# A fused attention and gated block on one core: w_phi loaded in 200-byte runs and placed by selection products, x tile 0 in halves, and a new order of work

## The chip, the cores and the metric

The kernel runs on one core of one Trainium2 chip. A core has five engines with instruction streams of their own: TensorE (PE, matrix products; its weight loads are shown apart as PEld), VectorE (DVE), ScalarE (ACT), GpSimd (POOL) and SyncE (SP, which here only issues transfers). Sixteen DMA engines move data; transfers are issued from SP's queue or from ScalarE's. The metric is the time of one execution on the device, in microseconds, as the median of several runs.

## The reference

x has 2048 rows of 640 columns; there are 32 heads of 20 columns, and F is 1536. All inputs are bf16.

```python
def A(x, wqkv, w_phi, wo):                # x is the layernorm of A_x
    q, k, v = split(x @ wqkv)             # 32 heads x 20
    pq, pk = q @ w_phi[h], k @ w_phi[h]   # 20 x 20 for each head
    phi_q = concat(softmax(pq), softmax(-pq))
    phi_k = concat(softmax(pk), softmax(-pk))
    kv, z = phi_k.T @ v, sum(phi_k)
    o = (phi_q @ kv) / (phi_q @ z + 1e-6)
    return merge_heads(o) @ wo

def B(x, w_gate, w_up, w_down):           # x is the layernorm of h
    return ((x @ w_gate) * (x @ w_up)) @ w_down

h  = x + A(layernorm(x), ...)
h2 = h + B(layernorm(h), ...)
```

## The kernel before

Rows are cut into 16 tiles t of 128; the 640 columns into five chunks c of 128 (`NC`). `build_graph` makes one `Op` for every piece of work, with its engine, the buffers it reads and writes, and a closure that emits the instructions; `G.op` takes its place from the table `PLAN`: a key that orders it on its engine, the number of the engine among the alternatives (`:1` moves it to the other one, for example a copy from ScalarE to VectorE, or a load from SP's queue to ScalarE's), and its buffer slots. `arrange` sorts each engine's operations by key, `emit` works out which semaphores each must wait for, and `program` emits them. So every queue runs strictly in the order of the table, and an operation that waits holds up all that stands behind it on its engine.

The stages, with the names that the text uses:

- **Loads** (`dma`, `xload`, `wrows`, `wqt`): x0, x1, x3 (one tile each), x4 to x14 (two tiles each), wk0 to wk4 and wv0 to wv4 (row chunks of the K and V parts of wqkv), w5 (w_phi as five chunks of 128 rows of 20 columns, that is 640 runs of 40 bytes), wqt0 to wqt4 (transposing loads of the Q part), wo, wg, wu, wd (the other weights).
- **Warm products** (L367, L372): `warm0` to `warm21` multiply a tile of zeros, eight first and then `NFILL` = 14, spread between the first real products.
- **Folds.** GpSimd multiplies w5 by a mask GL into the three block tensors Phi (`Ph0` to `Ph2`, L380). TensorE transposes the chunks of wk (`WT0` to `WT4`, L392), a copy brings each to SBUF (`WTe`), and the fold `F1_i` (L411) multiplies it with Phi, so that K is projected straight to pk; `Fe1_i` copies the result to `Wp` (L251). `F0_i` does the same for Q from wqt, once all five wqt are there.
- **Layernorm of x**: `L1s`, `L1a` (VectorE statistics), `L1l`, `L1e` (ScalarE), `xn` (L453). Tiles 0 and 1 are transposed by TensorE (`xt0`, `xt1`, L462; copies `xte`), the others by a transposing DMA from SP (`xt`, L471).
- **Projections** (L482): `K`, `V`, `Q` of a tile, ten products of about 320 columns each; for tiles 0 and 1 cut in five pieces of two products (`K0_0` to `K0_4`), by chunk of the weights.
- **Features of K**: two exponentials (`Kx`, L494), sums (`Ks`, L498), logarithm and exponential (`Kr`, `Ke`), the scaling (`Kn`, L518); then `KV` (L526), eleven products of 63 columns, accumulated over the 16 tiles. `KVe` masks the sum into KVm.
- **Q side**: `Qx`, `Qs`, `Qr`, `Qb`, `Qe`, `Qn`, and the transposing DMA `qT` (L575, on SP).
- **Output of attention**: `N` (L588, eleven products), division (`dd`, `rd`, `o`), transposing DMA `oT` (L619, on SP), `O` (L625), then `h`, `hc`, and the transposing DMA `hT` (L653, on SP).
- **Gated block**: row blocks 0 to 4 of 256, 512, 512, 512, 256 rows. `U{block}_{ft}_{0 or 1}` (L668) are the gate and up products, `g` and `u` their evacuation, `D{tile}_0` (L687) the down products, `y` the sum with the residual (L699), `w` the store (L701). The last tile, 15, is cut in three column pieces, `D15_0` (320), `D15_1` (224) and `D15_2` (96).

After the first folds the order on TensorE mixes the stages: K and V run with folds of Q and KV between them, the first N come after KV15, and the first U after O0 and O1.

Of the kernel before, what the change touches and what calls it, by code (L numbers as in the profile page):

```python
# [8 lines left out]
ALU = mybir.AluOpType  # L9
AX = mybir.AxisListType  # L10

P = 128
# [35 lines left out]
NFILL = 14  # L48
# [5 lines left out]
x1:0.78:1 ekz:0.78 x0:0.78 zero:0.91 id0:1.014 warm0:1.127 id1:1.252 x3:1.26:1 wk3:1.26:1 warm1:1.345 va1:1.496 warm2:1.564 w5:1.74:1 warm3:1.782 warm4:2.001  # L54
warm5:2.219 wk0:2.22:1 eps:2.326 gl0:2.357 warm6:2.437 gla:2.518 warm7:2.656 wk4:2.7:1 glb:2.822 warm8:2.874::0 warm9:3.093 wk1:3.18 warm10:3.311 warm11:3.529
wk2:3.66:1 L1s1:3.725 warm12:3.748 warm13:3.966 x4:4.14 warm14:4.185 warm15:4.403 L1s0:4.512 wv1:4.62 warm16:4.621 warm17:4.84 wv0:5.1:1 L1a1:5.299 L1s3:5.408
WT3:5.446::1 L1l1:5.532 wv2:5.58:1 Ph2:5.775 L1e1:5.858 warm18:5.902 warm19:6.011 wv3:6.06 WTe3:6.1:1 warm20:6.12 L1a0:6.195 xn1:6.304::0 Ph1:6.369 x2:6.54
WT0:6.546::2 L1l0:6.685 Ph0:6.761 L1a3:6.834 xt1:6.971::3 wv4:7.02:1 WTe0:7.023:1 L1l3:7.067 L1e0:7.249 WT4:7.25::4 L1e3:7.393 xte1:7.486 xn0:7.487::1 x6:7.5
L1n3:7.673 WT1:7.746::5 phz:7.897 WTe4:8.017:1 warm21:8.025 F1_0:8.134::6 WTe1:8.223:1 xn3:8.425::2 F1_3:8.453::0 WT2:8.772::2 Fe1_0:8.808:1 xt0:9.051::3
xt3:9.063 WTe2:9.249:1 F1_1:9.33::4 Fe1_3:9.392 F1_4:9.649::6 xte0:9.657:1 Fe1_1:9.976 L1s4:10.065 F1_2:10.153::0 x8:10.373 K0_0:10.472::2 Fe1_2:10.67:1  # L60
K0_1:10.743 L1s5:10.852 wqt4:10.853 K1_0:11.014::4 Fe1_4:11.254:1 K1_1:11.285 K1_2:11.556 L1a4:11.639 L1a5:11.762 V1_0:11.827::0 L1l4:11.995 K1_3:12.098
# [12 lines left out]
L1n10:34.156:1 L1a13:34.331 xn11:34.44::3 Kr4:34.517 Ve7:34.663::7 L1a15:34.97 xt11:35.078 L1a12:35.079 K9:35.091::6 Ks7:35.188::2 Ke4:35.247 Kx6_0:35.393::4
Kx6_1:35.977 Kn4:36.316 wd0:36.388 Q0_0:36.447::0 L1l12:36.561 Ks6:36.713::0 Q0_1:36.719 Kx9_0:36.743::1 Q0_2:36.991 Q0_3:37.263 Kr7:37.327 Q0_4:37.535
Ke7:37.618 L1e12:37.764 Q1_0:37.807::2 Kx9_1:37.857 Q1_1:38.079 xn10:38.106::2 Q1_2:38.351 Kr6:38.441 Q1_3:38.623 mk2:38.629 L1n12:38.636:1 Ke6:38.732
Ks9:38.811::3 Q1_4:38.895 L1n15:38.9 Kn6:39.123 KV4:39.167 Qx1_0:39.365::0 K8:39.5::6 Qx1_1:39.975 L1n13:40.204:1 xn13:40.488::0 Qx0_0:40.585::1 KV5:40.856
Qs1:41.018 xt13:41.126 Q5:41.189::2 Qx0_1:41.195 Kn7:41.437 Kx8_0:41.805::2 Kx8_1:42.389 xt10:42.436 xn15:42.453::1 K11:42.556::0 Kr9:42.973 Qx5_0:43.119::2
Ks8:43.125::1 Qr1:43.729::0 xt15:43.746 Ke9:43.875 KV6:43.912 Qx5_1:44.021 Qb1:44.073 Q3:44.245::6 Kn9:44.272 Qs0:44.518 Kx11_0:44.631::3 wu2:45.056
Kx11_1:45.215 wu3:45.536 KV7:45.612 Kr8:45.799 Q9:45.945::2 xn12:45.953::3 wu0:46.016 Ke8:46.09 Qx3_0:46.236::3 Ks11:46.483::0 wu1:46.496 Kn8:46.585  # L80
Qx3_1:46.846 K10:47.312::0 Qe1:47.456 Qx9_0:47.575::4 Qs3:47.876 Qx9_1:48.185 K15:48.668::6 Kr11:48.795 Qn1:48.898 Kx10_0:48.941::4 Qs9:49.311 Qr0:49.525::1
Qr3:49.671::2 Kx10_1:49.817 V8:50.024::2 Qb0:50.163 qT1:50.233::0 Qb3:50.362 Ke11:50.401 Kn11:50.735 Qs5:50.746 V9:51.38::0 Ve8:51.58::0 xt12:51.723
Kx15_0:52.164::0 Ks10:52.181::2 V13:52.736::2 Kx15_1:52.748 wo2:53.033 Qe3:53.332 Qe0:53.451 Ve9:53.57::1 L1n14:53.574:1 Qn3:53.639 xn14:53.858::0 V11:54.092::6
Ve13:54.292::4 Ks15:54.388::3 xt14:54.536 Qr9:54.876::3 Qn0:54.904 Qr5:55.022::0 Kr10:55.168 Q2:55.448::0 Ve11:55.648::2 Qb9:55.781:1 qT3:55.846::1 Qb5:56.169
Ke10:56.232 Kn10:56.566 KV8:56.815 Qx2_0:57.013::5 K13:57.148::2 qT0:57.336::2 Qx2_1:57.623 Kr15:58.233 Qe9:58.379 Qs2:58.418 Q4:58.504::6 Kx13_0:58.704::2
# [843 lines left out]
```

## Time and profile before

| | us |
|---|---|
| median of three runs | 271.86 (271.34 to 272.1) |
| span of the profiled execution | 270.1 |
| TensorE busy in it | 264.2 (98%) |
| VectorE, ScalarE, GpSimd busy | 160.0, 124.0, 71.3 |
| clock granted to TensorE | full in all 40 slices |

The span reaches from the first to the last instruction of the profiled execution; a time of that execution with what lies around the span is not recorded. The median of the runs is 1.76 us above the span. Engines are named by PE, PEld, DVE, ACT, POOL, and an engine's queue of transfers by SPq or ACTq. `ps` is PSUM; `scratch` holds the transposed weights of the folds and later the transposed features; `w` is w5; `ev` holds wk at first and the V tiles later; `Wp` holds the folded and V weights and later oT and the output tiles. A line such as "x10" counts instructions; "to landing" is the time from the issue of a transfer to its semaphore.

### The profile page before, as it was taken

Reading aid. Unit: us, or ns where it says so; the run is one execution under the profiler, and the core shown is the slowest. Engines: PE = TensorE matmul, PEld = TensorE weight load, DVE = VectorE, ACT = ScalarE, POOL = GpSimd, SP = SyncE. Lnnn points to the kernel's source line nnn. Section 1 sums busy time; section 2 is a strip of 40 time slices with the busy share of each in tenths; the row PEclk is TensorE's granted clock in tenths of the full one; section 3 lists DMA queues with packets and bytes.
Section 4 is the critical chain, followed back from the end, with each engine's and each line's share of the span. In section 5 each row is a group of like instructions: output and inputs, shape, how many; then the busy total and the mean of one; then the engine's idle time right before and its main releaser. Section 6 shows DMA issues by size and latency. Waiting matters only on the chain.

```text
span 270.1 us, 5186 instructions
## 1 busy us (share of the span) xinstructions
PE 264.2 (98%) x2092; PEld 177.9 (66%) x2105; DVE 160.0 (59%) x294; ACT 124.0 (46%) x316; POOL 71.3 (26%) x89
## 2 busy tenths in 40 slices
PE   7999999999999999999999999999999999999996
PEld 5777877777777788665556667765554476544774
DVE  4999799978988998577664253332342311423432
ACT  3899999988786382763540051222122300023000
POOL 4255689999923222205000000000000000000000
PEclk9999999999999999999999999999999999999999
DMA  7997995999958897973950001260200001100011
GB/s 200 318 168 136 249 222 129 302 183 245 204 106 143 163 126 149 140 123 64 171 93 2 0 0 36 57 106 1 73 12 2 0 0 51 49 1 0 27 49 61
DMA packets 71752, 28.09 MB, mean 104 GB/s; under 512 B 59056, under 2 KB 71728, under 8 KB 71728
## 3 DMA queue, kind: packets, MB, share of 16 engines
q1 hardware_dynamic: 71168, 27.10, 49.9%
q10 hardware_dynamic: 560, 0.66, 0.8%
q8 instruction: 16, 0.26, 0.4%
q14 instruction: 8, 0.07, 0.1%
HBM read 11.00 MB, written 2.62 MB: 50 GB/s over the span
## 4 chain that ended last, share of the span: by engine, by line
PE 90%; DMA 5%; DVE 2%; ACT 1%; issue 1%; SPq 1%; DVEq 0%
PE ps L668 36%; PE ps L482 24%; PE ps L687 19%; PE ps L625 6%; DMA scratch<-ph 2%; PE ps L526 2%; PE ps L588 2%; DMA Wp<-o 2%; DMA x_all<-in_A_x_dram 1%; PE ps L411 1%; SPq L653 1%; DVE st L428 0%; ACT Wp L251 0%; DVE st L429 0%; DVE ev L676 0%
## 5 line engine op out<-in xcount | busy, mean ns | idle before, releaser
L668 PE MATMUL ps<-xnT,Wgu 128*128 128x512 bf16 (+1 forms) x587 | 106.0, 335 | 0.7
L668 PEld LDWEIGHTS ps<-xnT,Wgu 128*128 128x128 bf16 x600 | 58.3, 98 | 43.4
L673 ACT ACTIVATE gt<-ps 128x512 bf16<-128x512 f32 (+1 forms) x60 | 29.7, 509 | 100.9 <-PE ps L668 62.9
L482 PE MATMUL ps<-Wp,xnT 128*128 128x320 bf16 (+1 forms) x480 | 68.6, 298 | 0.0
L482 PEld LDWEIGHTS ps<-Wp,xnT 128*128 128x128 bf16 x480 | 45.5, 97 | 17.2 <-issue 0.2
L676 DVE TENSOR_TENSOR ev<-ps,gt 128x512 bf16<-128x512 f32 (+1 forms) x60 | 33.6, 579 | 36.5 <-PE ps L668 27.8
L687 PE MATMUL ps<-Wd,ev 128*128 128x320 bf16 (+2 forms) x396 | 53.9, 295 | 0.0
L687 PEld LDWEIGHTS ps<-Wd,ev 128*128 128x128 bf16 x396 | 38.1, 98 | 15.3 <-DVE ev L676 0.2
L699 DVE SCALAR_TENSOR_TENSOR Wp<-ps,rs,x_all 128x640 bf16<-128x640 f32 (+3 forms) x18 | 14.6, 810 | 49.3 <-PE ps L687 49.1
L518 POOL TENSOR_TENSOR ek<-ek,SR 128x1280 bf16<-128x1280 bf16 x16 | 37.5, 2358 | 5.2 <-ACT SR L503 5.1
L551 ACT ACTIVATE ph<-ps 128x600 bf16<-128x600 f32 x32 | 21.4, 680 | 8.0 <-PE ps L482 6.9
L556 DVE TENSOR_REDUCE S<-ph 128x66 f32<-128x1320 bf16 x16 | 23.9, 1516 | 1.8 <-ACT ph L553 1.8
L625 PE MATMUL ps<-Wo,Wp 128*128 128x320 bf16 x160 | 23.9, 299 | 0.2
L498 DVE TENSOR_REDUCE SR<-ek 128x64 f32<-128x1280 bf16 x16 | 23.3, 1468 | 1.0 <-ACT ek L494 1.0
L570 POOL TENSOR_TENSOR ph<-ph,RQ 128x660 bf16<-128x660 bf16 x16 | 20.7, 1308 | 8.9 <-ACT RQ L566 8.9
L646 POOL TENSOR_SCALAR ln<-mv 128x1 f32<-128x1 f32 x12 | 2.3, 191 | 75.7 <-ACT ek L642 75.1
L494 ACT ACTIVATE ek<-ps 128x640 bf16<-128x640 f32 x32 | 21.2, 719 | 2.2 <-PE ps L482 1.5
L625 PEld LDWEIGHTS ps<-Wo,Wp 128*128 128x128 bf16 x160 | 15.3, 98 | 6.4 <-DMA Wp<-o 0.4
L631 DVE SCALAR_TENSOR_TENSOR x_all<-ps,x_all 128x640 bf16<-128x640 f32 x16 | 13.1, 821 | 6.4 <-PE ps L625 6.4
L615 DVE TENSOR_TENSOR o<-ps,sm 128x660 bf16<-128x660 f32 x16 | 13.4, 840 | 0.9 <-ACT sm L608 0.6
L642 ACT ACTIVATE ek<-x_all,mv 128x640 bf16<-128x640 bf16 x16 | 13.1, 821 | 0.0
L251 ACT ACTIVATE ev<-ps 128x640 bf16<-128x640 f32 x16 | 11.2, 704 | 1.1 <-PE ps L482 1.1
(69 smaller groups left out, 161.9 us busy)
## 6 DMA issues: line engine op xcount, KB each, us to landing
out_dram<-Wp SPq DMA_DIRECT2D x15, 160.0 KB, 1.8
Wgu<-in_B_w_gate_dram SPq DMA_DIRECT2D x4, 480.0 KB, 6.2
Wd<-in_B_w_down_dram SPq DMA_DIRECT2D x4, 480.0 KB, 4.7
Wgu<-in_B_w_up_dram SPq DMA_DIRECT2D x4, 480.0 KB, 5.6
x_all<-in_A_x_dram SPq DMA_DIRECT2D x5, 320.0 KB, 5.0
Wp<-in_A_wqkv_dram SPq DMA_DIRECT2D x5, 160.0 KB, 4.7
ev<-in_A_wqkv_dram SPq DMA_DIRECT2D x4, 160.0 KB, 4.2
x_all<-in_A_x_dram SPq DMA_DIRECT2D x3, 160.0 KB, 3.2
```

What stands on the lines that cost most here:

```text
L482: ins = e.matmul(pb(b, hb)[:, 0:n1 - n0], lhsT=T["xnT"][:, NC - 1 - c, P * t:P * (t + 1)], rhs=T["Wp"][:, POS[kind], c, n0:n1], start=(c = ...
L494: G.op("act", "%sx%d_%d" % (nm, t, s), lambda e, s=s, b=b, ek=ek: e.activation(out=T["ek"][:, ek.slots[0], 0:2 * D].rearrange("p (b h s f) ...
L498: G.op("dve", "%ss%d" % (nm, t), lambda e, ek=ek, sr=sr: e.tensor_reduce(out=T["SR"][:, sr.slots[0], 0, :], in_=T["ek"][:, ek.slots[0], 0: ...
L518: G.op("pool", "Kn%d" % t, lambda e, eng, ek=ek, sr=sr: e.tensor_tensor(out=T["ek"][:, ek.slots[0], 0:2 * D].rearrange("p (h f) -> p h f", ...
L551: e.activation(out=v[:, 0:10].rearrange("p (b g) j f -> p b g j f", b=2), in_=pp(b, 0, 300).rearrange("p b (g j f) -> p b g j f", j=3, f=D ...
L556: G.op("dve", "Qs%d" % t, lambda e, t=t, ph=ph: e.tensor_reduce(out=T["S"][:, t, 0:66].rearrange("p (g k) -> p g k", k=6), in_=pv(ph).rear ...
L570: return e.tensor_tensor(out=v, in0=v, in1=T["RQ"][:, rq.slots[0], 1, 0:33].rearrange("p (g j) -> p g j", j=3).unsqueeze(3).to_broadcast([ ...
L625: ins = e.matmul(pb(b, hb)[:, 0:320], lhsT=T["oT"][:, oT.slots[0], c, :], rhs=T["Wo"][:, c, 320 * hb:320 * (hb + 1)], start=(c == 0), stop ...
L668: ins = e.matmul(pb(b)[:, 0:n], lhsT=T["Wgu"][:, gu, c, P * ft:P * (ft + 1)], rhs=T["xnT"][:, NC - 1 - c, o0:o0 + n], start=(c == 0), stop ...
L673: G.op("act", "g%d_%d" % (bi, ft), lambda e, pg=pg, gt=gt, n=n: e.activation(out=T["gt"][:, gt.slots[0], 0:n], in_=pb(pg)[:, 0:n], func=AF ...
L676: o_ = G.op("dve", "u%d_%d" % (bi, ft), lambda e, pu=pu, gt=gt, hh=hh, ft=ft, n=n: e.tensor_tensor(out=T["hh"][:, hh.slots[0], ft, 0:n], i ...
L687: ins = e.matmul(pb(b, hb)[:, 0:w], lhsT=T["hh"][:, hh.slots[0], ft, P * tt:P * (tt + 1)], rhs=T["Wd"][:, ft, c0 + w * hb:c0 + w * (hb + 1 ...
```

## The change

The change has four parts and a new table.

1. `w5` loads w_phi as 128 rows of 200 bytes (partition p gets rows 5p to 5p + 4, as five groups j of 20 columns) into `w5r`. A selection matrix `ES` of 128 x 648 is zeroed on VectorE (`es0`) and gets its ones by an affine_select on GpSimd (`es1`). `W5` is 25 products of 128 x 128 by 128 x 20 on TensorE that place row r of w_phi on partition r mod 128 of chunk r div 128, and `W5e` copies the 100 columns from PSUM to `w5`, from where the Phi are made as before. `ES` and `w5r` lie in the slots of `gt`, which are used only much later.
2. x0 is loaded as two halves of 320 columns, `x0a` and `x0b`, with statistics of their own.
3. `NFILL` falls from 14 to 8.
4. `PLAN` is replaced; its keys are now the numbers 0 to 1029 in the order in which the operations are to start.

```diff
-NFILL = 14
+NFILL = 8
...
-    xload("sp", 0, 1, 0.7, also=["act"])
-    dma("act", "w5", lambda: T["w5"][:, :, :], lambda: T["A_wphi"].rearrange("h d f -> (h d) f").rearrange("(c p) f -> p c f", p=P), 160,
-        [w5_b], key=1.3, also=["sp"])
+    x0_b = [Buf("x0a"), Buf("x0b")]
...
+    for k, (e_, o_) in enumerate((("sp", "act"), ("act", "sp"))):
+        dma(e_, "x0" + "ab"[k], lambda k=k: T["x"][:, 0, 320 * k:320 * (k + 1)], lambda k=k: T["A_x"][0, 0:P, 320 * k:320 * (k + 1)], 82,
+            [x0_b[k]], key=0.7, also=[o_])
+    dma("act", "w5", lambda: T["w5r"][:, :, :].rearrange("p j f -> p (j f)"),
+        lambda: T["A_wphi"].rearrange("h d f -> (h d f)").rearrange("(p n) -> p n", p=P), 26, [w5r_b], key=1.3, also=["sp"])
...
+    G.op("dve", "es0", lambda e, eng: e.memset(T["ES"][:, :], 0.0), 0.40, LD, [], [es_b], -100, alts=[("pool", 0.7, LP)])
+    G.op("pool", "es1", lambda e: e.affine_select(out=T["ES"][:, :], in_=T["ES"][:, :], compare_op=ALU.not_equal, fill=1.0,
+                                                  base=-4, pattern=[[1, D + 8]], channel_multiplier=-5), 0.95, LP, [es_b], [es_b], -98.5)
...
+    b5 = Buf("pw5", "psum")
+    def w5s(e):
+        for c in range(NC):
+            for j in range(5):
+                ins = e.matmul(pb(b5)[:, DH * c:DH * (c + 1)], lhsT=T["ES"][:, P * c - j + 4:P * c - j + 4 + P], rhs=T["w5r"][:, j, :],
+                               start=(c == 0 and j == 0), stop=(j == 4), skip_group_check=True)
+        return ins
+    init["gt"] = [G.op("pe", "W5", w5s, 25 * 0.032, LT, [w5r_b, es_b], [b5], -92, before=wall)]
+    evac("W5e", lambda e, eng: copy(e, eng, T["w5"][:, :, :].rearrange("p c f -> p (c f)"), pb(b5)[:, 0:NC * DH]), 100, [b5], [w5_b], -91)
...
-    for t in range(NT):
+    st0_b = [Buf("st0a"), Buf("st0b")]
+    for k in range(2):
+        G.op("dve", "L1s0" + "ab"[k], lambda e, k=k: e.bn_stats(T["st"][:, 0, 6 * k:6 * k + 6], T["x"][:, 0, 320 * k:320 * (k + 1)]),
+             0.41, LD, [x0_b[k]], [st0_b[k]], -24)
+    G.op("dve", "L1a0", lambda e: e.bn_aggr(T["mv"][:, 0, :], T["st"][:, 0, :]), 0.11, LD, st0_b, [mv_b[0]], -25)
+    for t in range(1, NT):
```

Of the new table, the orders that the text speaks of (read from it by engine):

```
TensorE, start, before: warm0-17 WT3 warm18-20 WT0 xt1 WT4 WT1 warm21 F1_0 F1_3 WT2 xt0 F1_1 F1_4 F1_2 K0_0 K0_1 K1_0 ...
TensorE, start, after:  warm0-9 W5 warm10 WT1 warm11-12 WT0 warm13 WT2 warm14 WT3 F1_1 warm15 F1_2 F1_0 xt0 WT4 xt1
                        K0_0 F1_3 K1_0 K0_1 F1_4 K0_2 K1_1 K1_2 V0_0 K0_3 K0_4 V1_0 V1_1 V0_1 K1_3 K1_4 V0_2 V0_3 V1_2
                        V1_3 V1_4 V0_4 K3 F0_2 F0_1 V5 K2 F0_0 V3 V2 F0_4 K5 F0_3 KV0 ...
TensorE, middle, before: KV15 Q6 N0 N2 Q7 N1 Q11 N9 Q8 N3 Q14 N5 O0 O2 O1 N4 O9 O3 Q12 N7 Q15 U0_1_0 ...
TensorE, middle, after:  KV15 Q6 N0 N2 Q7 N9 N1 Q8 N3 O0 O2 N5 N10 O1 Q11 O9 O3 Q14 U0_2_0 ...
TensorE, end, before: ... D14_0 D11_0 D13_0 D12_0 D10_0 D15_1 D15_2
TensorE, end, after:  ... D14_0 D15_0 D15_2 D10_0 D12_0 D13_0 D11_0 D15_1
ScalarE, start, after: x0b w5 wk1 x0a x3 wk2 W5e WTe1 WTe0 L1l1 L1l0 L1e1 L1e0 L1l3 L1e3 Fe1_1 Fe1_2 xte0 xte1 xn3 Fe1_3 ...
VectorE, start, after: zero es0 L1s0b L1s1 L1s2 L1s0a L1a1 L1s3 L1a0 L1a3 WTe2 WTe3 xn0 L1a2 xn1 Fe1_0 WTe4 ...
GpSimd, start, after: eps id0 gl0 id1 gla es1 ekz phz glb Ph0 Ph2 Ph1 L1n3 Sz ...
SP, start, before: x0 x3 w5 wk0 wk4 wk1 wk2 x4 wv1 wv0 wv2 wv3 x2 wv4 x6 xt3 x8 wqt4 wqt1 xt5 wqt0 xt2 wqt2 xt4 wqt3 ...
SP, start, after:  x1 x2 wk0 wk3 wqt4 wk4 x6 x4 wv0 wv1 wqt3 wv3 wv2 wqt1 x8 wv4 xt3 wqt0 wqt2 xt5 xt2 x14 wo0 xt4 ...
SP, middle, after: ... qT5 qT2 qT10 oT0 oT2 oT1 oT9 oT3 qT4 hT0 ...
```

More of the change, by code (lines that the diff above doesn't have):

```diff
@@ L58 @@
[L58 to L61, printed above, removed]
@@ new lines @@
+wk3:21 warm6:22 x3:23 warm7:24 wqt4:25 warm8:26::5 ekz:27 warm9:28 wk2:29 L1s0b:30 phz:31 L1s1:32 W5:33::0 wk4:34:1 glb:35 x6:36 L1s2:37 warm10:38 W5e:39
+WT1:40::1 x4:41 warm11:42 Ph0:43 L1s0a:44 WTe1:45:1 warm12:46 WT0:47::7 wv0:48:1 L1a1:49 Ph2:50 warm13:51 L1s3:52 WTe0:53 wv1:54 WT2:55::1 Ph1:56 wqt3:57
+L1l1:58 warm14:59 L1a0:60 L1a3:61 WT3:62::0 WTe2:63:1 L1l0:64 L1e1:65 F1_1:66::6 L1e0:67 L1l3:68 WTe3:69 warm15:70 L1e3:71 F1_2:72::1 xn0:73::3 Fe1_1:74
+wv3:75 L1n3:76 F1_0:77::4 Sz:78 L1a2:79 xn1:80::1 Fe1_2:81:1 wv2:82:1 xt0:83::0 WT4:84::6 Fe1_0:85 wqt1:86 xte0:87 xt1:88::7 xte1:89 WTe4:90:1 K0_0:91::4
```

170 lines of the change are left out of this document (77 added, 93 removed).

## The prediction

> **What bounds the kernel now.** I read first the busy time of the engines in three stretches (length, then busy time of TensorE, its weight loads, VectorE, ScalarE and GpSimd, granted clock, DMA share, GB/s), then the chain of waits in order of time (start, length, what), then the waits of TensorE between 80 and 125 us (total, times, longest).
>
> ```profile
> 0.00:10.70 10.70, 8.55 (x89) 6.66 (x89) 6.81 (x19) 6.05 (x13) 5.34 (x18) 1.00 0.84 262
> 10.70:267.70 257.00, 255.60 (x2005) 171.23 (x2016) 152.91 (x275) 117.94 (x303) 65.94 (x71) 1.00 0.50 97
> 267.70:270.10 2.40, 0.00 (x0) 0.00 (x0) 0.32 (x1) 0.00 (x0) 0.00 (x0) 1.00 0.33 102
> ```
>
> ```profile
> 10.70 14.95 PE ps L482 x110
> ...
> 25.65 0.64 PE ps L411 x12
> ...
> 29.32 0.67 PE ps L526 x22
> 30.00 1.36 PE ps L482 x10
> 31.36 0.32 PE ps L411 x6
> ...
> 91.53 0.33 PE ps L588 x11
> ...
> 249.64 18.05 PE ps L687 x144
> ...
> 267.78 0.32 DVE Wp L699
> ```
>
> ```profile
> PE ps L588 <- DMA scratch<-ph: 0.4, 1, 0.4
> PEld ps L625 <- DMA Wp<-o: 0.4, 1, 0.4
> ```
>
> From 10.70 us, where the chain turns into one run of K and V products, to 267.70 TensorE is busy 255.60 of 257.00 us. Of the missing 1.40 part is no wait: 2005 products are recorded against 2016 weight loads, so 11 records are lost. Two real waits show, 0.4 us each, one of N products on a qT transpose and one of an O on an oT transpose, together 0.8. The change alters no product after 10.70 us in number or shape. So the time has three parts: the start, the waits in 257 us, the 2.4 us after the last product. The new order can win 0.8 to 1.4 in the middle at most; it can lose any amount there, because no later slack of TensorE takes a wait back. ScalarE, VectorE and GpSimd matter through what they release.
>
> **The start, part by part.** Timeline rows, then landings by DMA (KB, us from issue):
>
> ```profile
> 1.12 1.89 PE L367 MATMUL ps<-ev 128*128 128x256 bf16 x8 [1.12 <-DVE ev L365]
> ...
> 1.26 0.45 ACTq L285 DMA_DIRECT2D ev<-in_A_wqkv_dram  x1
> ...
> 1.72 0.43 SPq L285 DMA_DIRECT2D w<-in_A_w_phi_dram  x1
> ...
> 2.80 2.34 PE L372 MATMUL ps<-ev 128*128 128x256 bf16 x10
> ...
> 6.13 1.68 POOL L380 TENSOR_TENSOR Phi<-w,GL 128x280 bf16<-128x280 bf16 x3 [2.47 <-DMA w<-in_A_w_phi_dram]
> ...
> 8.04 0.80 PE L411 MATMUL ps<-Phi,scratch 128*128 128x140 bf16 x12
> ...
> 8.78 3.26 ACT L251 ACTIVATE Wp<-ps 128x640 bf16<-128x640 f32 x5
> ```
>
> ```profile
> w<-in_A_w_phi_dram SPq DMA_DIRECT2D x1, 25.0 KB, 4.3
> x_all<-in_A_x_dram ACTq DMA_DIRECT2D x1, 160.0 KB, 3.1
> ev<-in_A_wqkv_dram ACTq DMA_DIRECT2D x1, 160.0 KB, 3.6
> ```
>
> Before, w_phi is issued at 1.72 and lands 4.3 later, at 6.0; GpSimd, which had waited 2.47 us for it, makes the three Phi by 7.81 (6.13 + 1.68), and the first fold follows at 8.04. After, the load is second in ScalarE's queue, at about 1.26. A whole 160 KB load issued there at that time took 3.6, the first of that queue 3.1; 25 KB between them lands at 4.4 to 4.9, I take 4.6. Then come 25 products of 20 columns. The nearest product is L526: 22 in 0.67, 30 ns each, so 0.78 us at full rate. But the start doesn't run at full rate (mean ns of a product on zeros, first in 4.0 to 4.6 us, then in 5.2 to 6.0):
>
> ```profile
> L372 PE MATMUL ps<-ev 128*128 128x256 bf16 x5 | 1.3, 421 | 0.0
> ...
> L372 PE MATMUL ps<-ev 128*128 128x256 bf16 x3 | 0.5, 272 | 0.0
> ```
>
> The same product takes 421 ns early and 272 later, although the clock column reads 1.00 in all stretches; the faster ones come after the 18 products that fill 1.12 to 5.14. I take 1.2 us for the 25, with 0.78 and 1.56 as ends. The Trainium skill, "TensorE: Matmul & The Clock Gate", Part 1, says that the array runs at half rate until about 3.4 us of sustained products have passed; the trace agrees, with a change of rate about 4 us after the first. By that rule the 25 products take their 1.56.
>
> After the change only ten products on zeros stand ahead of W5: at 0.21 us each (8 from 1.12 to 2.80) they end at 3.3, and TensorE then waits for w_phi. That the rate then stays low is a rival below.
>
> So W5 ends at 4.6 + 1.2 = 5.8. Its copy out of PSUM on ScalarE, 100 columns, isn't in the trace: below the 0.65 of a 640-column copy (3.26 / 5), with the signals 0.3. Then the same three Phi, 1.68: done at 7.8. So the shorter runs buy nothing at the folds; the products and the copy take the 1.4 us back. Ends: 6.9 to 8.7.
>
> The selection matrix: its zeros lie on VectorE before x has landed and cost nothing (less than the 0.65 of a 640-column copy if that cover went: 3.26 / 5). Its affine_select on GpSimd isn't in the trace:
>
> ```profile
> 1.47 0.29 POOL L335 TENSOR_SCALAR_AFFINE_SELECT ident<-ident 128x128 bf16<-128x128 bf16 x1 [0.23 <-POOL ident L332]
> ...
> L570 POOL TENSOR_TENSOR ph<-ph,RQ 128x660 bf16<-128x660 bf16 x16 | 20.7, 1308 | 8.9 <-ACT RQ L566 8.9
> ```
>
> 128 columns took 0.29 and another operation on 660 took 1.31; I take 0.9 for 648: begun behind five short ones at about 2, it is done by 3, ahead of the load. Behind it wait only the memsets and glb, done before Phi. Halving x0 leaves the same bytes; the second half is fourth in ScalarE's queue and xn0 stands behind two copies of transposed weights on VectorE anyway: nothing, and 0.3 if it landed after them. The six products on zeros that go lay in waits: nothing.
>
> From the first fold, at 7.9, the order asks of ScalarE two fold copies and the copy of xt0 (0.65 each) before K0_0 may run: 7.9 + 0.32 + 0.3 + 1.95 = 10.45, against 10.70. But two folds, F1_3 and F1_4, then still stand among the K products, 2 x 0.32. The start comes to -0.25 + 0.64 = **+0.4**; with the ends of Phi, and with wk2 landing early or late, -0.3 to +1.1. ScalarE's wk2 and SP's wk4 stand behind x2 and the transposing load wqt4; only WT2, WT4 and what TensorE has queued behind them wait for those, and that is inside the range.
>
> **The Q folds come forward.** F0_2 runs after K3, at about 18 us (10.45 + 1.6 + 6.0, below) where the first Q folds ran at 25.65, and needs all five wqt. The fifth, wqt2, is issued as third transpose after xt3 in SP's queue, with xt5 and xt2 behind it, for which V5 and K2 wait. (Line, count, ns min/median/max; then landing.)
>
> ```profile
> L309 SPq DMA_TRANSPOSE scratch<-in_A_wqkv_dram x5: 1167/1271/2227, 11.1 to 21.2; - x5
> ...
> DMA to landing us min/median/max: 3.2/4.2/5.0
> ```
>
> xt3 is issued about when K0_2 starts (both follow the copy of xt1, one by 0.9 of other products, one by the 0.9 of xn3). From there to F0_2 stand 17 pieces of two products at 0.136 (14.95 / 110) and K3, 4.62 + 1.36 = 6.0 us. wqt2 goes out 2 x 1.27 after xt3, so 3.45 us are left, and landing takes 3.2, 4.2 or 5.0. Wait: 0 to 1.55; I take **+0.6**, near the median's 0.75. V5 and K2 come behind and are covered by it.
>
> **The first O.** Timeline rows of the first N products and the first oT, then the landing of oT:
>
> ```profile
> 74.74 0.84 PE L588 MATMUL ps<-KVm,scratch 128*128 128x63 bf16 x22
> ...
> 77.32 2.60 SPq L619 DMA_TRANSPOSE Wp<-o  x2
> ...
> DMA to landing us min/median/max: 2.6/2.7/4.7
> ```
>
> Between the start of N0 and O0 stood six N and four Q, 6 x 0.33 + 4 x 1.36 = 7.4 us; now five N and two Q, 4.4. N0 to the issue of oT0 took 2.5 us here (VectorE's division, then SP), the landing 2.7: 5.2. TensorE waits 0.8 at O0. With qT10 just ahead of oT0 in SP's queue, up to 2.8; with a later N0 on the same chain, 0. I take **+0.8**.
>
> **The first block of gates.**
>
> ```profile
> 82.30 4.24 PE L625 MATMUL ps<-Wo,Wp 128*128 128x320 bf16 x30
> ...
> 88.17 2.60 SPq L653 DMA_TRANSPOSE xnT<-xn  x2
> ...
> DMA to landing us min/median/max: 2.6/2.7/4.5
> ```
>
> O1 ended at 86.54 and hT1, the second of these two, was issued at 89.5 and landed 2.7 later: 5.7 us. Between O1 and the first U now stand Q11, O9, O3 and Q14, 5.44 us: **+0.2**, 0 to 2.0.
>
> **Elsewhere.** The two waits of before stand at places that the new order lays out anew. I let half of them go, **-0.4**, between -0.8 and as much again of new ones.
>
> **The end.**
>
> ```profile
> 267.20 0.90 DVE L699 SCALAR_TENSOR_TENSOR Wp<-ps,rs,x_all 128x224 bf16<-128x224 f32 x2 [0.27 <-PE ps L687]
> ...
> out_dram<-Wp SPq DMA_DIRECT2D x1, 56.0 KB, 1.6
> out_dram<-Wp SPq DMA_DIRECT2D x1, 24.0 KB, 1.4
> ```
>
> The last product was the 96-column piece; now it is the 224-column one, so the last store is the 56 KB one: 1.6 instead of 1.4, **+0.2**, 0 to 0.4.
>
> **Sum.** 0.4 + 0.6 + 0.8 + 0.2 - 0.4 + 0.2 = +1.8 us on the span of 270.1. The runs' median, 271.86, lies 1.76 above the span (no time around the profiled execution is recorded); I carry that difference: 273.7.
>
> **Rivals.**
> *Transposes land at their shortest* (wqt2 3.2, oT 2.6), and both old waits go: 0.4 + 0 + 0.7 + 0.1 - 0.8 + 0.2 = +0.6, 272.4. For it: SP is free of loads by 12 us. Against it: the wqt of before had a median of 4.2.
> *Faster: the transposes run ahead of TensorE.* One mechanism, on SP's queue: with wqt out early and x2 in front, each transpose is issued before TensorE needs it, and of the 1.40 us all but the lost records' share, say 1.2, goes. Start -0.1, end +0.2: -1.1, 270.8. It decides at O0: oT0 must land within 4.4 us of N0, where 5.2 were taken; the whole chain before it must be 0.8 shorter. Against it is that even the least landing, 2.6, leaves 5.1.
> *The half rate lasts.* It is what the rule of "TensorE: Matmul & The Clock Gate" in the Trainium skill would bring. With ten products on zeros and then a wait, TensorE keeps 421 ns instead of 272 beyond 5 us. WT3 and the first fold lie on the path, 0.3 us more each; if it lasts to 12, the K products there lose another 0.7: +1.3 on the sum, 275.0. For it: the fast rate came only after 4 us of unbroken products. Against: later the rate held over a start that is busy 8.55 of 10.70.
>
> **How the numbers follow.** Forecast 0.44, its own range 272.7 to 274.9; short landings 0.27; faster 0.16; half rate 0.13. A difference of 0.3%, 0.8 us, is about what a measurement here can tell from none. Faster 0.16, same 0.27, slower 0.44 + 0.13 = 0.57. The range, 271.1 to 276.4, leaves out the better half of the faster case and the far ends of the slower ones.
>
> **What would show it.** Right: a first K product at 10.2 to 10.9; a wait of L411 on the scratch load near 18 us; a wait of L625 on the o transpose between the first N and the first O; a last store of 56 KB. Wrong: Phi finished before 7 us, folds begun at once and K0_0 before 9.8; F0 and O0 without a wait; or products of 421 ns after 6 us.

## The result, and the profile after

The changed kernel takes 281.7 us (median of four runs, 280.83 to 283.06) where that of before takes 271.6 (270.98 to 272.1) beside it: ratio 1.038, 95% interval 1.034 to 1.042. Slower, as forecast, but by 10 us instead of 1.8. The profiled execution has a span of 281.3, 11.2 more than the 270.1 of before. It is the slowest of the four (283.06 us); the other three have spans of 279.0 to 280.2 and a mean granted clock of 1.00, where it has 0.994.

The busy time by stretch of after (length, then TensorE, its weight loads, VectorE, ScalarE, GpSimd, granted clock, DMA share, GB/s), cut at the first K product and at the last product:

```profile
0.00:14.45 14.45, 9.66 (x94) 7.60 (x94) 7.46 (x20) 6.19 (x14) 4.97 (x19) 1.00 0.95 232
14.45:30.00 15.55, 15.53 (x135) 11.48 (x136) 15.19 (x36) 14.73 (x33) 5.11 (x6) 1.00 0.85 187
30.00:60.00 30.00, 28.66 (x291) 21.21 (x289) 28.42 (x37) 26.59 (x73) 22.00 (x23) 1.00 0.88 210
60.00:79.00 19.00, 19.00 (x182) 14.06 (x180) 18.77 (x14) 16.42 (x47) 15.31 (x8) 1.00 0.64 111
79.00:90.00 11.00, 7.97 (x104) 5.88 (x101) 6.33 (x15) 3.85 (x14) 4.09 (x4) 0.84 0.85 130
90.00:278.22 188.22, 187.26 (x1317) 120.24 (x1329) 91.21 (x185) 57.64 (x142) 11.30 (x22) 1.00 0.32 62
278.22:281.30 3.08, 0.01 (x1) 0.00 (x0) 0.89 (x2) 0.00 (x0) 0.00 (x0) 1.00 0.22 72
```

Three parts again. The start: 14.45 instead of 10.70, and two folds of 0.32 still to come, +4.4. The middle, last product minus first K product minus those folds: 278.22 - 14.45 - 0.64 = 263.13 against 257.0, **+6.1**. The end: 3.08 against 2.40, +0.7. Sum 11.2. In the middle TensorE stands still for 1.34 us at 30 to 60 and 3.03 at 79 to 90, and VectorE has hardly any room from 14 to 79 us. Three stretches of before that hold about the same work on TensorE, for comparison:

```profile
10.70:26.00 15.30, 15.30 (x120) 11.09 (x119) 14.95 (x32) 13.79 (x32) 6.04 (x9) 1.00 0.98 174
26.00:56.00 30.00, 30.00 (x305) 22.55 (x303) 27.91 (x42) 28.61 (x78) 26.39 (x23) 1.00 0.95 209
56.00:73.00 17.00, 17.00 (x185) 12.81 (x184) 14.14 (x11) 14.87 (x44) 16.45 (x11) 1.00 1.14 241
```

VectorE was nearly as full before up to 56 us, but had 2.86 us of 17 left ahead of the first N, where it now has 0.23 of 19; GpSimd had done 26.39 us of work in the second stretch, now 22.00. TensorE's waits from 12 to 125 us (total, times, longest), then the chain of waits into the first N products:

```profile
PE ps L592 <- DMA scratch<-ph: 2.0, 1, 2.0
PE ps L486 <- DMA xnT<-xn: 1.3, 2, 0.8
PE ps L530 <- POOL ek L522: 1.0, 1, 1.0
PE ps L672 <- issue: 0.3, 1, 0.3
```

```profile
67.83 4.67 POOL ek L522 x2
72.50 1.26 POOL ph L574
73.76 5.73 POOL ek L522 x2
79.49 5.31 DMA scratch<-ph
84.84 0.64 PE ps L592 x11
85.49 2.67 PE ps L486 x10
```

Before, this chain was TensorE alone from 10.70 to 83.8 us, past the first N, with some transposes on it later; now GpSimd's products on K and then the transpose of a Q tile lead into N. The waits have new names too: no F0 waits for a transposing load, no O for oT. Ten products of Q took 1.37 before; here 2.67, on which more below. The waits come to 4.6, with 1.3 for these slow products 5.9, against 0.8 before: 5.1 of the 6.1. The 1.3 belong to this one execution: the slow products run at a granted clock of 0.50, and the mean clock of 1.00 in the other three leaves no room for that. The start, by the timeline:

```profile
1.75 0.45 ACTq L265 DMA_DIRECT2D ev<-in_A_wqkv_dram  x1
3.19 0.45 ACTq L265 DMA_DIRECT2D ev<-in_A_wqkv_dram  x1
4.36 0.84 PE L370 MATMUL ps<-gt 128*128 128x20 bf16 x25 [0.92 <-DMA gt<-in_A_w_phi_dram]
5.57 1.68 POOL L379 TENSOR_TENSOR Phi<-w,GL 128x280 bf16<-128x280 bf16 x3 [1.93 <-ACT w L230]
7.04 0.71 PE L391 MATMUL ps<-ident,ev 128*128 128x128 bf16 x5 [1.62 <-DMA ev<-in_A_wqkv_dram]
7.66 0.49 DVE L427 BATCH_NORM_STATS2 st<-x_all 128x6 f32<-128x320 bf16 x1 [1.84 <-DMA x_all<-in_A_x_dram]
9.85 0.72 PE L391 MATMUL ps<-ident,ev 128*128 128x128 bf16 x5 [0.92 <-DMA ev<-in_A_wqkv_dram]
10.60 0.49 DVE L230 COPY scratch<-ps 128x640 bf16<-128x640 bf16 x1 [0.71 <-PE ps L391]
```

Phi is ready at 7.25, earlier than before. What is late is wk: wk1, issued at 1.75, starts its transpose at 7.04, and wk2, issued at 3.19, at 9.85 (before, the first of them ran at 4.93 and the third and fourth at 7.37). A whole load of wk on ScalarE's queue took 5.9 us in the median, where one took 3.6 before.

### The profile page after: what moved, and what is told of

It is laid out like the page before. It is cut to its first block, busy times and chain, and to the rows that moved or that the text cites. A ratio compares the mean times of both kernels' runs of the same rounds, so it can differ in the third digit from the quotient of the medians.

```text
span 281.3 us, 5222 instructions
## 1 busy us (share of the span) xinstructions
PE 268.1 (95%) x2110; PEld 180.5 (64%) x2124; DVE 168.3 (60%) x303; ACT 125.4 (45%) x320; POOL 62.8 (22%) x79
## 4 chain that ended last, share of the span: by engine, by line
PE 75%; DMA 9%; DVE 5%; POOL 4%; ACT 3%; issue 2%; ACTq 1%; DVEq 0%
PE ps L672 37%; PE ps L691 17%; PE ps L486 11%; PE ps L629 7%; DMA xnT<-xn 4%; POOL ek L522 4%; DMA ev<-in_A_wqkv_dram 2%; PE ps L592 2%; DMA scratch<-ph 2%; DVE SR L502 1%; DMA out_dram<-Wp 1%; ACT ek L498 1%; PE ps L410 1%; DVE S L560 1%; DVE xn L457 1%
## 5 line engine op out<-in xcount | busy, mean ns | idle before, releaser
L486 PE MATMUL ps<-Wp,xnT 128*128 128x320 bf16 (+1 forms) x480 | 70.4, 302 | 1.6 <-DMA xnT<-xn 1.3
L522 POOL TENSOR_TENSOR ek<-ek,SR 128x1280 bf16<-128x1280 bf16 x14 | 34.7, 2488 | 13.0 <-ACT SR L507 12.9
L574 POOL TENSOR_TENSOR ph<-ph,RQ 128x660 bf16<-128x660 bf16 x11 | 14.6, 1326 | 40.4 <-ACT RQ L570 40.4
L230 ACT ACTIVATE ev<-ps 128x640 bf16<-128x640 f32 x14 | 9.8, 712 | 2.2 <-PE ps L486 2.2
```

What stands on the lines that cost most here:

```text
L486: ins = e.matmul(pb(b, hb)[:, 0:n1 - n0], lhsT=T["xnT"][:, NC - 1 - c, P * t:P * (t + 1)], rhs=T["Wp"][:, POS[kind], c, n0:n1], start=(c = ...
L522: G.op("pool", "Kn%d" % t, lambda e, eng, ek=ek, sr=sr: e.tensor_tensor(out=T["ek"][:, ek.slots[0], 0:2 * D].rearrange("p (h f) -> p h f", ...
L574: return e.tensor_tensor(out=v, in0=v, in1=T["RQ"][:, rq.slots[0], 1, 0:33].rearrange("p (g j) -> p g j", j=3).unsqueeze(3).to_broadcast([ ...
```

## The experiments

Times are medians; the ratio is to the kernel of before beside it, with its 95% interval. "Order of after up to X" means that the table holds the operations of after up to X in their order, and then those left in the order and with the buffer slots of before (the first free slot where that of the table is still in use).

**The parts without the order.** The code of after under the table of before; then with 14 products on zeros; then with w_phi loaded first.

```diff
 b2_parts:     PLAN of before; W5 4.9, W5e 5.0, x0a 0.78, x0b 0.79:1, es0 0.95, es1 1.4
 b3_parts14:   the same, and
-NFILL = 8
+NFILL = 14
 b4_w5_first:  as b2_parts, and w5 from SP at 1.74 to ScalarE at 0.77
```

> The old order with the three parts of code: w_phi in 200-byte runs with the 25 selection products, x0 in halves, 8 instead of 14 filling products on zeros (warm16 to warm21 go). Theory (the order makes the whole loss): within 1 us of before. Rival (the parts cost, by the half rate or by the longer way to Phi): 1.5 us or more slower.

> The changed code under the order of before, as in the last such run (273.3, first product of the K run at 12.4), but with the 14 waiting products on zeros of before in place of 8. If the half rate of TensorE's start makes the 1.5 us of that run, the transposes of wk and the folds run at full rate by 8 us, the K products start at about 11.0, and the time is 272.0. If it is the longer way to Phi (25 products and a copy behind the load of w_phi), the K products still start at 12.0 or later, and the time is 273.0 to 273.5.

> The new parts under the order of before (273.3), with the load of w_phi first in ScalarE's queue instead of third in SP's. Theory: Phi is then done at 7.2 instead of 9, the folds are no longer behind before's, the first K product is at 10.5 to 11, and the time that of before, 272 (ratio 0.998 to 1.002). Rival: the folds wait for the transposed weights, whose loads and x1 now stand behind it, or for the half rate; the first K product is at 12, and the time 273 or more.

b2 took 273.31 (1.0049, 1.0024 to 1.0075), b3 273.84 (1.0057, 1.0023 to 1.0091), b4 272.13 (1.0019, 0.9991 to 1.0047). The first K products of b2, b3 and b4:

```profile
12.44 7.83 PE L510 MATMUL ps<-Wp,xnT 128*128 128x320 bf16 x56
```

```profile
12.45 7.77 PE L510 MATMUL ps<-Wp,xnT 128*128 128x320 bf16 x56
```

```profile
11.87 8.37 PE L509 MATMUL ps<-Wp,xnT 128*128 128x320 bf16 x60
```

More products on zeros change nothing, so their number isn't what sets this start. b2's loss lies between its theory (1 us) and its rival (1.5). With w_phi first, no difference from before is measured, though the first K product is at 11.87, not at 10.5 to 11 where the theory had it; its time came out right and its reason didn't. The parts cost some 1.3 us, half a per cent, and little or nothing when their load is first; of the 10 us the order makes the rest.

**The transposing load at the start.** wqt4 behind the other loads in after; wqt4 early in before.

```diff
 a1_wqt_late:   in after,  wqt4 25 -> 98.2, wqt3 57 -> 98.4, wqt1 86 -> 98.6
 b1_wqt_early:  in before, wqt4 10.853 -> 2.5
```

> The changed kernel with wqt4, wqt3 and wqt1 moved behind the last plain load (wv4) in SP's queue. Theory (transposing loads among the weight loads make wk late): wk2 lands near 7 us instead of 9.8, the first K product is at 11 instead of 14.45, the time falls by 2.5 to 3.5 us. Rival (the start is late by the half rate of TensorE after too few products on zeros): wk may land earlier, but the folds still run at half rate and the first K product stays above 13; at most 1 us. Rival (the plain loads in two queues share the bandwidth): wk2 still lands after 9.

> The kernel before with one transposing load, wqt4, moved up between wk0 and wk4 in SP's queue. Theory: wk4, wk1 and wk2 land 1.5 to 3 us later, and the time rises by 1.5 to 3 us. Rival (the transposing load is one more 160 KB load, 0.45 us of bandwidth): within 0.6 us.

a1: 282.9 (1.0406, 1.0347 to 1.0466), with wk1's transpose still at 7.14 and the first K product at 14.52. b1: 272.55 (1.0021, 1.0001 to 1.0041). The transposing load doesn't make wk late.

**Which stretch of the order costs.**

```diff
 h1_start:  order of after up to K0_0, then before's
 h1_folds:  order of after up to KV0, then before's
 h2_late:   order of before up to N0, then after's
 h3_out:    order of before up to U0_4_0 (the first gates), then after's
```

> The order of after up to the first K product, all that is left then in the order of before (with the new parts; the same parts under the order of before alone took 273.3). Theory: the start of after costs what its first K product is later (14.4 instead of 12.4), and behind it TensorE stays busy: 275.3. Rival: the late start also puts VectorE and GpSimd back, which do not catch up, and TensorE waits again before the first N: 278 or more.

> The order of after up to the first KV product, which takes in the five Q folds that came forward, then that of before. Theory: the five fold copies (0.70 us each) stand on ScalarE ahead of K's exponentials, GpSimd begins at 26 and TensorE waits before the first N: 278 to 280, 3 or more above the run with only the start of after. Rival: the folds are neutral where they stand, and the time is that of the other run, 275.3.

> The order of before up to the first N product, that of after from there on (with the new parts; 273.3 with the order of before throughout). Theory: the late half is neutral but for its tail, where the last y waits for a store: 273.3 + 0.7 = 274.0. Rival: the new order of gates, O products and stores costs by itself, with the O waits of the prediction: 276 or more.

> The order of before up to the first gates of the first block (about 93 us), that of after from there (with the switch at the first N the time was 277.7, with a wait of 2.5 us for a transposed Q tile and half rate after it). Theory: the blocks, gates and stores are neutral in the new order, and the loss of the late half lies between the first N and the first gates: 273.5 to 274.2. Rival: it lies in the O products and late Q tiles among the gates: 276 or more.

| order of after | us | ratio (95%) |
|---|---|---|
| nowhere (b2) | 273.31 | 1.0049 (1.0024 to 1.0075) |
| to K0_0 | 275.71 | 1.0123 (1.0090 to 1.0156) |
| to KV0 | 279.79 | 1.0263 (1.0232 to 1.0293) |
| throughout (after) | 281.7 | 1.0381 (1.0342 to 1.0419) |
| from N0 | 277.66 | 1.0197 (1.0166 to 1.0228) |
| from U0_4_0 | 277.36 | 1.0189 (1.0152 to 1.0226) |

By the ratios, times 271.6: the parts 1.3, the start 2.0, from the first K to the first KV 3.8, all after it 3.2. The start alone is as the theory said. In h1_folds the time is the theory's too, but not by the theory's wait ahead of the first N: the loss is one wait at 30 to 40 us, and the clock column falls behind it (waits; then stretches):

```profile
PE ps L501 <- DMA xnT<-xn: 2.2, 1, 2.2
```

```profile
30.00:40.00 10.00, 7.84 (x73) 5.53 (x72) 7.81 (x14) 6.17 (x14) 6.75 (x8) 0.93 1.02 272
40.00:50.00 10.00, 10.00 (x99) 7.15 (x97) 6.37 (x12) 8.43 (x24) 7.15 (x6) 0.90 0.73 146
```

The late half costs 4 us by itself: there the rivals held. Each of the two runs has one long wait of TensorE close behind its own switch from one order to the other (2.55 us, N3 behind the exponentials of a Q tile, at 83 us; 2.46 us, gates, at 99), so part of their loss may belong to the seam; how much of it after has at the same place they don't tell. The same holds for h1_folds: its wait of 2.2 us is that of K7, the first projection behind KV0 and KV1, where the order is that of before again. After itself waits 0.56 us for an x tile behind its KV0, and its own trace has its long waits at 79 to 90. So the 3.8 and 3.2 are prices of these joined orders, not of the two stretches in after.

**The start, in more detail.** The wk loads first and all on SP; then, on the start alone, also the sums over x2 and x3 behind the copies of the transposed weights.

```diff
 c1_wk_first:   in after, SP: x1, wk1, wk0, wk2, wk3, wk4, x2, wqt4, ...; ScalarE: x0b w5 x0a x3
 h1_start_fix:  h1_start with the same, and L1s3, L1a3 51, 61 -> 74.5; L1s2, L1a2 37, 79 -> 86.5
```

> After, with the five loads of wk in one queue, SP's, behind x1 and ahead of x2, the transposing load, x4 and x6. Theory: the late K products (14.5) come from wk1 and wk2 that stand in ScalarE's queue and share the DMA engines with SP's loads; with them first the last wk lands by about 7.5, the first K product is at 11.5, and 2.5 to 3 us of the time go: 278.8. Rival: the half rate and the order of ScalarE's copies set the start; wk lands early, but the first K product stays above 13.3, and the time is 281 or more.

> The start of after and the rest of before, as in the run that took 275.7, with the five loads of wk first in SP's queue and the sums over x2 and x3 behind the copies of the transposed weights on VectorE. Theory: the start is late through two things, wk in two queues, and VectorE's copies of the transposed weights behind sums that wait for x2 and x3; with both mended the first K product is at 12 or before and the time 273.3, as with the whole order of before. Rival: the start's three fold copies ahead of the K products set it, and the time stays 275 or more.

c1: 282.04 (1.0347, 1.0310 to 1.0384). h1_start_fix: 274.87 (1.0110, 1.0081 to 1.0139). Rows of c1:

```profile
5.05 0.74 PE L393 MATMUL ps<-ident,ev 128*128 128x128 bf16 x5
7.99 0.74 PE L393 MATMUL ps<-ident,ev 128*128 128x128 bf16 x5
8.67 0.49 DVE L434 BATCH_NORM_STATS2 st<-x_all 128x6 f32<-128x320 bf16 x1 [3.80 <-DMA x_all<-in_A_x_dram]
10.97 0.83 DVE L232 COPY scratch<-ps 128x640 bf16<-128x640 bf16 x2
14.24 0.74 PE L488 MATMUL ps<-Wp,xnT 128*128 128x320 bf16 x2
```

The four transposes now start from 5.05 to 7.99 instead of 7.04 to 10.57: the place of wk in the queues was what made them late. But VectorE stood for 3.8 us at the sums of x2 with the copies of the weights behind it, and K began no earlier. With that mended too K still began at 13.97 (14.60 in h1_start), and the chain of waits from 8.95 to 13.60 is VectorE's normalisations, sums and copies one after the other. The start is bound twice, by loads and by VectorE's order; no run here mended both fully.

**The features of K.** The 13 operations that the table gives to VectorE put on GpSimd; the logarithm and exponential of K0, K1, K3 early; all repairs with another output slot; all with more.

```diff
 a2_gpsimd:  in after, Qb0 1 2 4 6 8, Qn0 1 5 7 14, Kn9 11: VectorE -> GpSimd
 c2_kfeat:   in after, Ke0 179 -> 156.5; Kr1, Ke1 196, 204 -> 166; Kr3, Ke3 187, 194 -> 176; Kn0, Kn1, Kn3 behind them
 c3_all:     c1_wk_first + c2_kfeat + w15_0 1024 -> 1017.5, y12 ahead of y13, y11 slot 1 -> 0, y15_1 slot 0 -> 1
 c4_fix:     c3_all + a2_gpsimd + the sums over x2, x3 as in h1_start_fix + qT2 449 -> 441.5, ahead of qT5
```

> The changed kernel with the 13 Qb, Qn and Kn that its table gives to VectorE back on GpSimd, at the same places of the order. Theory (products of VectorE with both operands in SBUF wait while GpSimd runs one of its own, and hold the queue): the idle time of TensorE between 30 and 90 us falls from 4.4 to under 2 and the time by 2 to 3 us. Rival (GpSimd has no room for them, and KV wait for Kn): TensorE waits as long or longer, the time is the same or up to 3 us more. Rival (the late start alone made the middle late): no change within 1 us.

> After, with the Ln and Exp of K0, K1 and K3 placed in ScalarE's order as soon as their sums are made, ahead of the copies of the Q folds, so that GpSimd's products on K begin earlier. Theory: GpSimd begins its first at 22 to 23 instead of 26.6 and ends the last of the 16 at 73 to 74 instead of 77.3; TensorE's idle 3 us at 79 to 90 shrinks below 1, and 2.5 to 4 us of the time go: 278.5. Rival: the late products on K are a follower of VectorE and ScalarE, which are full from 30 to 79; GpSimd begins earlier, but N0 still waits for its transpose until 84 to 85, and the time is 281 or more.

> After, with the loads of wk first, the early Ln and Exp of K0, K1 and K3, and at the tail another slot of the output buffer for y11 (0, whose store is issued earlier) with y12 ahead of y13 on VectorE. Theory: the three add up, 2.8 + 3.2 + 0.7: 275.0, with the store wait of 2.3 us before the last y gone. Rival: the middle is a fixed chain (engines full), so that only start or tail show: 278 to 281.

> After with all repairs together: wk loads first in one queue; the sums over x2 and x3 moved on VectorE behind the copies of the transposed weights (with the loads alone moved, VectorE waited 3.8 us for x2 ahead of them); the early Ln and Exp of K0, K1, K3; the 13 operations back on GpSimd; the transpose of ph2 ahead of that of ph5 in SP's queue; the other output slot at the tail. Theory: the start then gives 2.5 us (first K product at 12.0), the middle 3, the tail 0.7: 275.5. Rival: the middle is bound by ScalarE, which has the fold copies to do among K's features in any case: the time is 279 or more although the first K product is at 12.

a2 284.07 (1.0465, 1.0406 to 1.0524), c2 282.87 (1.0383, 1.0331 to 1.0435), c3 282.48 (1.0366, 1.0326 to 1.0406), c4 283.34 (1.0383, 1.0335 to 1.0432): all four are misses for the theory. First products on K on GpSimd, of after and of c2; then the waits of a2 and c4:

```profile
26.56 4.77 POOL L522 TENSOR_TENSOR ek<-ek,SR 128x1280 bf16<-128x1280 bf16 x2 [6.12 <-ACT SR L507]
```

```profile
21.97 7.07 POOL L524 TENSOR_TENSOR ek<-ek,SR 128x1280 bf16<-128x1280 bf16 x3 [1.94 <-ACT SR L509]
```

```profile
PE ps L532 <- POOL ek L524: 3.8, 2, 2.7
```

```profile
PE ps L534 <- POOL ek L526: 3.6, 2, 2.7
```

With the operations on GpSimd, GpSimd is the full one (18.47 of 19 us at 60 to 79) and KV waits for it; with them on VectorE, VectorE is. Three products on K 4.6 us sooner didn't end the 16 sooner, since the tiles that follow are late: c2 waits 3.0 us for transposed x tiles instead of 1.3. A wait that was removed came back at the next place. Only the tail gave what was expected in kind: the last product of c3 is at 277.80, 2.6 before the end instead of 3.08, and no y waits for a store.

**What the stretch from K to KV is.** h1_folds with the Q folds where before had them; the folds alone put forward under the order of before; and h1_folds_late with the bias of the normalised tiles on VectorE.

```diff
 h1_folds_late:   h1_folds, F0_*, Fe0_* and what is left in the order of before
 b5_folds_early:  b4_w5_first, wqt4 2.5, wqt3 6.2, wqt1 7.6, wqt0 10.85, wqt2 12.16; F0_2 15.7, F0_1 18.7, F0_0 21.4, F0_4 22.75, F0_3 24.1, Fe0_* 0.9 behind
 h1_nb_dve:       h1_folds_late, L1n*: VectorE
```

> The order of after up to the first KV product and then that of before, as in the run that took 279.8, but the five Q folds and their copies stay where before had them. Theory: the folds' copies on ScalarE ahead of K's features are what the run lost against the 275.7 of the start alone; the time falls to 276 or 277, and the wait of 2.2 us for a transposed x tile at 30 to 40 us goes. Rival: it is the order of K, V, x tiles and weight loads in that stretch, or the late Ln and Exp of K0 and K1; the time stays at 279 or more.

> The new parts under the order of before with w_phi loaded first (272.1), and the five Q folds with their copies put forward among the K and V products of tiles 2 to 5, as after has them, with their transposing loads ahead. Theory: the folds forward cost 1 us by themselves, through ScalarE's copies: 273.0 to 273.5. Rival: they cost nothing under an order in which K's features start at 17 us: 272.1 (ratio 0.999 to 1.003). Second rival: they cost 3 us or more, and the order of K and V is innocent: 275.

> The run that took 278.4 (order of after up to the first KV, Q folds where before had them), with the small operation that makes the bias of the normalised x tiles (0.26 us) on VectorE for all tiles. In that run ScalarE's normalisation of a tile waits at 34 us behind three products on K of GpSimd (7 us), because the small operation stands behind them. Theory: this is a part of the stretch's loss; the wait of TensorE for transposed tiles at 24 to 40 us falls from 2.4 to about 1 and the time to 277. Rival: the tile is late in any case, through VectorE's sums; the time stays at 278 or above.

h1_folds_late: 278.35 (1.0225, 1.0200 to 1.0251). b5: 278.14 (1.0237, 1.0212 to 1.0263). h1_nb_dve: 278.23 (1.0241, 1.0207 to 1.0275). Waits of b5 from 10 us on:

```profile
PE ps L509 <- ACT Wp L253: 2.1, 3, 0.8
PE ps L433 <- ACT SR L530: 1.2, 1, 1.2
PE ps L553 <- POOL ek L545: 0.9, 1, 0.9
```

The folds forward are not free: 6 us alone under the order of before, more than any of the three expectations. But 2.1 of that is products that waited for a fold's copy because this table gave all folds one pair of PSUM banks, which after does not; the rest is a fold behind ScalarE's work, late x tiles and a late product on K. Taking them back out of after's order won only 1 us (intervals 1.0232 to 1.0293 and 1.0200 to 1.0251 overlap), and that 1 us may be the clock: all four executions of h1_folds have a mean granted clock of 0.994, all four of h1_folds_late 1.00. So the order of K, V, x tiles and loads loses some 3 us without them, in these joined orders. The place of the small bias operation is not it. Which order within the stretch does it is **left open**. No version beat before.

## Why the prediction was wrong

The direction and the main reason (no slack of TensorE takes a lost microsecond back) held; the sum of terms fell short by 9 of 11 us.

- **Start, forecast +0.4, measured +4.4.** The costed chain came out well and didn't matter: w_phi landed 3.0 after its issue (3.3 taken), the 25 products took 0.84 (1.2), Phi was done at 7.25 (7.8). The step that failed is the sentence that wk2 and wk4 behind other loads are "inside the range", at most some tenths. (It misread the queue, too: wk2 stands behind x0a and x3 on ScalarE's, not behind x2.) wk1 and wk2 were the limit, by 2 to 3 us, and behind them, as c1 and h1_start_fix show, VectorE's order of sums and copies. I counted what stands ahead in each queue, not that loads of two queues run beside each other. (That they slow each other is argued from the landings, 5.9 against 3.6; c1 changed queue and place at once.)
- **x0 in halves, "nothing, and 0.3".** The sums of its second half began at 7.66, where before, by the timeline, VectorE had begun them at 5.11. In h1_start_fix they are done at 7.35, ahead of the chain that sets its start at 8.95 to 13.60, so there the halves cost nothing. In after their price wasn't measured.
- **First Q folds, +0.6 for wqt2.** No such wait. What the folds cost, if anything, is not their own wait. b5 points at their five copies, which ScalarE does among K's exponentials, and at their loads ahead of x tiles; in after neither is shown. I had costed the products' wait alone.
- **First O, +0.8; first U, +0.2.** No O waits for oT; the first U shows 0.3. N waits 2.0 us for qT2 instead: it stands in SP's queue behind qT5, and so behind a scaling on VectorE that took 2.99 us. I had looked at qT10 ahead of oT0, not at the transposes ahead of N.
- **"Elsewhere", -0.4.** The other step that failed. I let old waits go and wrote no term for new ones. The trace of after shows 4.6 us of them instead of 0.8: 1.3 for x tiles, 1.0 for a product on K of GpSimd, 2.0 for qT2, 0.3 at the first U. What I think lies behind them is engines that get full: eleven operations on K and Q moved from GpSimd to VectorE (of the 13, Qb2 and Qb4 were there before), which is then busy 18.77 of 19 us ahead of N, and GpSimd's first product on K is at 26.6 instead of 16.8, behind ScalarE's new order. That is argued, not shown: a2 took the operations off VectorE and c2 put GpSimd's start forward, and neither won time. Which engine's order makes these waits stays open.
- **End, +0.2, measured +0.7.** The 56 KB store is the smaller part; y11 reuses an output slot whose store is under way:

```profile
277.87 1.24 DVE L703 SCALAR_TENSOR_TENSOR Wp<-ps,rs,x_all 128x640 bf16<-128x640 f32 x2 [2.27 <-DMA out_dram<-Wp]
```

Of the rivals, the half rate came true in its condition (transposes of five products take 0.71 to 0.74 until 12 us, and 0.44 at 13.5), but b3 doesn't support its price, and in h1_start_fix the rate was full from 9 us on and K began at 13.97 all the same. In after itself the chain from 9.85 to 13.69 us is TensorE at the low rate. The first normalised tile was done at 12.35 (11.75 + 0.60, VectorE), and its transpose began at 13.11, so a full rate could have brought that forward by at most some 0.8 us; this is an estimate from those rows, and no run tests it. The rivals asked only how transposes land, and what the rate is; none asked which engine gets full.

## What to carry to other kernels

When a whole order is replaced, add up each engine's work stretch by stretch, not only TensorE's, and list what each first consumer waits for; an engine with no room left can't make up a delay, and here a repair at one place moved the wait to the next. A full engine alone tells little: before, ScalarE was busy 28.61 of 30 us and TensorE waited for nothing. Loads that the start needs can go into one queue ahead of all others (c1 had the transposes 2 us sooner by it), but what stands behind a late tile on an in-order engine counts with them, and there the 2 us were lost again. Orders can be bisected: the order of one up to an operation, that of the other from there. The price of a stretch that comes out takes in the wait at the seam, so look in the trace whether the whole order has that wait at all.

## What the runs showed of the hardware

**A wait of about 2 us can cost the rate behind it, and need not.** Products of after around N, then of h2_late, then of c1:

```profile
80.99 1.53 PE L486 MATMUL ps<-Wp,xnT 128*128 128x300 bf16 x10
84.84 0.64 PE L592 MATMUL ps<-KVm,scratch 128*128 128x63 bf16 x11 [1.99 <-DMA scratch<-ph]
85.32 2.84 PE L486 MATMUL ps<-Wp,xnT 128*128 128x300 bf16 x10
```

```profile
82.96 0.51 PE L607 MATMUL ps<-KVm,scratch 128*128 128x63 bf16 x11 [2.55 <-ACT ph L572]
83.31 4.55 PE L644 MATMUL ps<-Wo,Wp 128*128 128x320 bf16 x20
91.11 2.88 PE L644 MATMUL ps<-Wo,Wp 128*128 128x320 bf16 x20
```

```profile
85.62 0.51 PE L594 MATMUL ps<-KVm,scratch 128*128 128x63 bf16 x11 [2.13 <-DMA scratch<-ph]
85.98 1.53 PE L488 MATMUL ps<-Wp,xnT 128*128 128x300 bf16 x10
```

Behind waits of 1.99 and 2.55 us the same products take nearly twice as long, 1.3 and 1.7 us more in all, at a granted clock of 0.50. Behind 2.13 us in c1 they don't, nor behind 1.78 in c2. So the length of the wait alone doesn't decide it: by the mean clock, all four executions of h2_late were slowed (0.988 to 0.994), but only one of the four of after (0.994, the others 1.00). The Trainium skill, "TensorE: Matmul & The Clock Gate", Part 1, has the array fall to half rate after an idle window of about 3.4 us; here less than that was enough in two of these traces.

**VectorE and GpSimd stretch each other.** Durations in ns (min/median/max), in after, of the scaling of Q on GpSimd and on VectorE and of the products on K on GpSimd; then of the latter before:

```profile
L574 POOL TENSOR_TENSOR ph<-ph,RQ x11: 1304/1305/1528, 59.2 to 147.9; 128x660 bf16<-128x660 bf16 x11
L574 DVE TENSOR_TENSOR ph<-ph,RQ x5: 835/1601/2994, 49.2 to 158.8; 128x660 bf16<-128x660 bf16 x5
```

```profile
L522 POOL TENSOR_TENSOR ek<-ek,SR x14: 2353/2357/3601, 26.6 to 77.3; 128x1280 bf16<-128x1280 bf16 x14
```

```profile
L518 POOL TENSOR_TENSOR ek<-ek,SR x16: 2353/2357/2367, 16.8 to 69.9; 128x1280 bf16<-128x1280 bf16 x16
```

An operation that moved from GpSimd (1.31) to VectorE took up to 2.99 there, from 75.03 us on, while GpSimd was at two products on K from 73.72 to 80.24, one of which took 3.60; no data pass between them. With the 13 operations on GpSimd (a2) none of its products on K took more than 2.37. The Trainium skill, "GPSIMD Engine Reference", Specifications, says that the engine's access to SBUF is shared with VectorE's operations of two SBUF inputs; the rows agree.
